# Finer transfers of w2, and the small loads cut so that the output's transfer takes the last of eight semaphores

## The chip, the cores and the metric

One core of one Trainium2 chip. The metric is device time of one execution in microseconds (us). The kernel before took 355.64 us (median of 3 executions, 355.63 to 355.8). Every execution also has a span (first to last instruction; 1.7 to 3.1 us shorter) and a mean granted TensorE clock. One execution of each kernel leaves a trace, and all trace times below are counted from the start of its span. PE is TensorE, DVE VectorE, ACT ScalarE and SP the sync engine. A transfer has landed when the last of the DMA engines that carry it has reported. The hidden vector is `relu(h @ w1)`, and the drain is the sync engine's first instruction after its final waits.

## The reference

One decode step of an adaptive-norm block: the modulation vectors come from `c`, attention reads a cache of 32768 keys and values for 8 groups of heads, and a small feed-forward layer follows.

```python
mod = (silu(c) @ w_mod).reshape(1, 6, 1, -1)        # sa, ca, ga, sb, cb, gb
h = layernorm(x) * (1 + ca) + sa
x = x + ga * attention(h, k_cache, v_cache, wq, wo)  # 8 groups, 32768 x 128 each, bf16
h = layernorm(x) * (1 + cb) + sb
x = x + gb * (relu(h @ w1) @ w2)                     # 512 -> 1792 -> 512
```

Nine tenths of the 149.42 MB that are read (134.2 MB) are the cache. The weights w1 and w2 (1.8 MB each) are read last.

## The kernel before

All loads go through one queue, issued by the sync engine (SP) in a fixed order: w_mod (`wm`), c, x, wq, then K and V, wo, w1, w2. Four large buffers in SBUF go round. The parts that the change and the argument touch:

```python
# w2 in six transfers: (first row pair, row pairs, which rows of the pair); FB = 2, FA = 7
W2P = [(0, 2, slice(0, FB)), (2, FA - 5, slice(0, FB)), (FA - 3, 1, slice(0, FB)), (FA - 2, 1, slice(0, FB)),
       (FA - 1, 1, slice(0, 1)), (FA - 1, 1, slice(1, FB))]
W1P = [(0, KT - 1), (KT - 1, KT)]
# ... cut ...
w2_v = B_w2.rearrange("(a p b) d -> p a b d", p=P, b=FB)   # pair a: 256 KB, 2 KB on each partition
# ... cut ...
wm_sb = need(("wm",))
cx_row = const.tile([16, D // 8], BF16)
stream_dma(cx_row[0:8], c[0].rearrange("(a n) -> a n", a=8))
stream_dma(cx_row[8:16], A_x[0, 0].rearrange("(a n) -> a n", a=8))
# ... cut: attention, projection, second norm, w1 ...
for part, (base, n, bs) in enumerate(W2P):
    w2_sb = need(("w2", part))          # each part's first matmul waits for that part's transfer
    for a in range(n):
        for b in range(bs.start, bs.stop):
            ft = (base + a) * FB + b
            for i in range(KT):         # 4 matmuls per row tile, 56 in all
                nc.tensor.matmul(ffn_ps, lhsT=hid_bd[:, ft, i, :], rhs=w2_sb[:, a, b - bs.start, i*P:(i+1)*P], ...)
# two vector operations, then
nc.sync.dma_start(out=out[0, 0].rearrange("(i n) -> i n", i=KT), in_=o_bf[:])
```

Two rules are not in the code but in the built program. Each transfer takes the next of eight semaphores in turn, and waits until the transfer eight before it has landed. And the program ends with six waits of the sync engine on all semaphores, in a fixed order: 2; 3 and 1; 4 and 0; 5; 6; 7.

## Time and profile before

| | before |
|---|---|
| time | 355.64 us |
| span of the profiled execution | 353.7 us |
| DMA queue, share of 16 engines | 98.4% |
| PE / DVE busy | 79% / 59% |
| last transfer of w2 landed | 350.20 |
| last matmul started | 350.49 |
| output landed, then drain of the sync engine | 352.531, 352.845 |

The kernel is bound by the bytes it reads. The prediction shows the lines for that.

### The profile page before, as it was taken

How to read it: one execution, taken by the hardware profiler on the slowest of the kernel's cores; microseconds unless marked ns; L12 is line 12 of the kernel's file. 1: busy time of each engine (PE TensorE's matmuls, PEld its weight loads, DVE VectorE, ACT ScalarE, POOL GpSimd, SP SyncE). 2: the span in 40 equal slices, each digit the busy share in tenths (PEclk: the TensorE clock that was granted, in tenths of full speed). 3: DMA queues.
4: the chain of work that ended last, by engine and by line, in shares of the span. 5: the costliest groups of instructions: out<-in, count | busy, mean ns of one | idle time of the engine just before them, and what ended most of it. 6: DMA issues, size and time to landing. Idle time of an engine off the chain costs nothing. (4 is left out here: it accounts for less than half of the span.)

```text
span 353.7 us, 4064 instructions
## 1 busy us (share of the span) xinstructions
PE 278.1 (79%) x1348; PEld 111.8 (32%) x1351; DVE 207.3 (59%) x269; ACT 28.2 (8%) x68; POOL 8.5 (2%) x14
## 2 busy tenths in 40 slices
PE   0352781999898979897969797979789787989995
PEld 0121230333343423332323233333333233334445
DVE  8555774882868268472949177553938095743050
ACT  1212004000110011001100101010100010020000
POOL 9000000000000000000000000000000000000000
PEclk9995997799899999999999998999999999999999
DMA  8999999999999999999999999999999999999994
GB/s 317 450 419 452 432 412 437 448 419 424 459 419 422 445 437 421 437 441 419 437 448 419 424 459 416 426 436 437 422 434 445 426 424 448 430 422 422 423 418 186
DMA packets 7076, 149.59 MB, mean 423 GB/s; under 512 B 792, under 2 KB 1048, under 8 KB 2200
## 3 DMA queue, kind: packets, MB, share of 16 engines
q1 hardware_dynamic: 7064, 149.43, 98.4%
q8 instruction: 8, 0.13, 0.1%
q14 instruction: 4, 0.03, 0.0%
HBM read 149.42 MB, written 0.00 MB: 422 GB/s over the span
## 5 line engine op out<-in xcount | busy, mean ns | idle before, releaser
L411 DVE STREAM_TRANSPOSE KTt<-Ksb 128x2048 f32<-128x2048 f32 x64 | 143.2, 2283 | 66.5 <-DMA Ksb<-in_A_k_cache_dram 58.8
L493 PE MATMUL o_ps<-Vsb,PT_g 128*16 (+1 forms) x512 | 128.0, 382 | 22.4 <-ACT qbd L395 9.5
L431 PE MATMUL S_ps<-KTt,qbd 128*128 128x512 bf16 x512 | 122.5, 391 | 22.2 <-DVE KTt L411 20.6
L431 PEld LDWEIGHTS <-qbd 128*128 128x128 bf16 x512 | 49.0, 98 | 87.0 <-issue 29.1
L493 PEld LDWEIGHTS o_ps<-Vsb,PT_g 128*16 x416 | 35.9, 86 | 90.7 <-issue 66.4
L437 DVE TENSOR_SCALAR_CACHE_REDUCE S_g<-S_ps 128x512 f32<-128x512 f32 x16 | 11.0, 690 | 27.7 <-PE S_ps L431 27.7
L395 ACT COPY qbd<-qrep_sb 32x128 bf16<-32x128 bf16 x32 | 9.4, 295 | 139.0 <-PE S_ps L431 137.9
L474 DVE STREAM_TRANSPOSE PT_g<-P_g 128x1024 bf16<-128x1024 bf16 x8 | 9.7, 1218 | 6.6 <-ACT P_g L468 6.6
L465 ACT ACTIVATE nbias<-Mb_ps 128x1 f32<-128x1 f32 x8 | 1.4, 171 | 131.1 <-PE Mb_ps L463 131.1
L493 PEld LDWEIGHTS <-PT_g 128*16 128x16 bf16 x96 | 8.2, 90 | 11.0
L233 PE MATMUL xc_ps<-cx_sel,cx_bd 16*128 16x2 bf16 x4 | 0.3, 172 | 12.8 <-DVE cx_bd L227 12.8
L468 ACT ACTIVATE P_g<-S_g,nbias 128x1024 bf16<-128x1024 f32 x8 | 9.2, 1148 | 0.2
L524 DVE SCALAR_TENSOR_TENSOR Y<-o_ps,smask,Y 16x128 f32<-16x128 f32 x24 | 8.1, 339 | 0.8
L179 DVE COPY sel<-ident_bf 128x128 bf16<-128x128 bf16 x4 | 7.6, 3730 | 0.0
L480 PE MATMUL L_ps<-Lexp,ones_f 128*128 128x4 f32 x16 | 3.0, 257 | 4.3 <-DVE Lexp L477 4.3
L606 PE MATMUL spare_ps<-qbd,ident_bf 128*128 128x512 bf16 x16 | 5.1, 380 | 0.2 <-issue 0.2
L449 PE MATMUL mT_ps<-ident_f,m_p 128*1 128x128 f32 x8 | 2.2, 270 | 3.9 <-DVE m_p L446 2.0
L452 DVE TENSOR_REDUCE Mrow<-mT_ps 1x4 f32<-1x128 f32 x8 | 2.1, 257 | 5.3 <-PE mT_ps L449 5.3
L480 PEld LDWEIGHTS L_ps<-Lexp,ones_f 128*128 128x128 f32 x16 | 3.1, 222 | 5.7 <-issue 5.1
L543 DVE TENSOR_TENSOR oT_sb<-acc_ps,Linv 128x4 bf16<-128x4 f32 x8 | 1.2, 151 | 5.7 <-PE acc_ps L530 5.7
L514 DVE MEMSET o_ps<- 16x512 f32 x8 | 3.9, 485 | 0.8
L561 DVE CAST o_sb<-o_ps 128x4 bf16<-128x4 f32 (+2 forms) x4 | 0.7, 166 | 6.1 <-PE o_ps L557 6.1
(112 smaller groups left out, 85.2 us busy)
## 6 DMA issues: line engine op xcount, KB each, us to landing
Ksb<-in_A_k_cache_dram SPq DMA_DIRECT2D x16, 4096.0 KB, 29.2
Vsb<-in_A_v_cache_dram SPq DMA_DIRECT2D x15, 4096.0 KB, 24.5
wq_sb<-in_A_wq_dram SPq DMA_DIRECT2D x1, 4096.0 KB, 18.8
Vsb<-in_A_v_cache_dram SPq DMA_DIRECT2D x2, 2048.0 KB, 23.4
wm_sb<-in_w_mod_dram SPq DMA_DIRECT2D x1, 3072.0 KB, 10.4
wo_sb<-in_A_wo_dram SPq DMA_DIRECT2D x1, 2048.0 KB, 25.1
w_sb<-in_B_w_dram SPq DMA_DIRECT2D x1, 1344.0 KB
wo_sb<-in_A_wo_dram SPq DMA_DIRECT2D x1, 1024.0 KB, 27.0
```

Source lines behind the costliest of these rows:

```text
L179: nc.vector.tensor_copy(out=sel[:, hp, :].rearrange("p (a c) -> p a c", a=4), in_=src)
L395: nc.scalar.copy(out=o, in_=i)
L411: t = nc.vector.transpose(out=KTt[:].bitcast(F32), in_=Ksb[:, 32 * half:32 * half + 32, :].rearrange("p j d -> p (j d)").bitcast(F32),)
L431: nc.tensor.matmul(S_ps_tiles[g], lhsT=qbd[g % 2][:, hp, s, :], rhs=KTv[:, 16 * sl:16 * sl + 16, h, :, par], start=(t4 == 0 and sl == 0 an ...
L437: nc.vector.tensor_scalar(out=S_tiles[g][:, G, :], in0=S_ps_tiles[g], scalar1=1.0, scalar2=None, op0=ALU.mult, op1=ALU.max, accum_out=m_ti ...
L468: nc.scalar.activation(out=P_g[:], in_=S_g[:].rearrange("p g f -> p (g f)"), func=ACT.Exp, bias=nbias[:], scale=scale, accum_out=l_g[:],)
L474: nc.vector.transpose(out=PT_g[:], in_=P_g[:])
L480: nc.tensor.matmul(L_ps[:], lhsT=ones_f[:], rhs=Lexp[:], start=True, stop=True)
L493: nc.tensor.matmul(o_tiles[g][:], lhsT=PT, rhs=Vx, start=False, stop=False, skip_group_check=True)
L514: nc.vector.memset(o_tiles[g][:], 0.0)
L524: nc.vector.scalar_tensor_tensor(out=Y[:], in0=o[:, s], scalar=smask[:, s:s + 1], in1=Y[:], op0=ALU.mult, op1=ALU.add,)
L606: nc.tensor.matmul(spare[0], lhsT=ident_bf[:], rhs=qbd[0][:, 0, 0:4, :], start=True, stop=True)
```

## The change

The intent: matmuls of w2 can begin on each row pair as it lands, and the output's transfer is the 56th, so that its semaphore is the last one that the final waits ask for.

```diff
-    W2P = [(0, 2, slice(0, FB)), (2, FA - 5, slice(0, FB)), (FA - 3, 1, slice(0, FB)), (FA - 2, 1, slice(0, FB)),
-           (FA - 1, 1, slice(0, 1)), (FA - 1, 1, slice(1, FB))]
+    W2P = [(a, 1, slice(0, FB)) for a in range(FA - 1)]
+    W2P += [(FA - 1, 1, slice(b, b + 1)) for b in range(FB)]
...
-    stream_dma(cx_row[0:8], c[0].rearrange("(a n) -> a n", a=8))
-    stream_dma(cx_row[8:16], A_x[0, 0].rearrange("(a n) -> a n", a=8))
+
+    for at, row in ((0, c[0]), (8, A_x[0, 0])):
+        rows = row.rearrange("(a n) -> a n", a=8)
+        for a0, a1 in ((0, 3), (3, 6), (6, 8)):
+            stream_dma(cx_row[at + a0:at + a1], rows[a0:a1])
```

## The prediction

> **What bounds the kernel now.** I read the page from its second part down. The DMA row of the forty slices says which resource is full, and it is full nearly everywhere:
>
> ```profile
> DMA  8999999999999999999999999999999999999994
> ...
> q1 hardware_dynamic: 7064, 149.43, 98.4%
> ```
>
> The reader is to see that the sixteen DMA engines are nine tenths busy or more in 38 of 40 slices, and that the one queue through which all loads go fills 98.4% of them. The table of stretches (columns: bounds and length of the stretch, busy time of PE, PEld, DVE, ACT, POOL with instruction counts, granted clock, DMA share, GB/s) gives the rate between start-up and tail:
>
> ```profile
> 20.00:340.00 320.00, 262.54 (x1146) 102.00 (x1145) 190.30 (x219) 23.99 (x61) 0.00 (x0) 0.96 1.00 431
> ```
>
> DMA share 1.00 at 431 GB/s, while PE works 262.54 of 320 us. So nothing that only starts a load earlier helps in the middle: the bytes (149.42 MB) set the time. What the change can touch is the first 20 us and the last few. The chain that ended last shows those:
>
> ```profile
> 305.94 25.65 DMA Vsb<-in_A_v_cache_dram
> 331.59 0.02 issue
> 331.61 16.67 DMA w_sb<-in_B_w_dram
> 348.28 0.04 issue
> 348.32 2.41 PE ffn_ps L742 x40
> 350.73 0.02 issue
> 350.75 0.29 DVE o_rows L747
> ```
>
> Loads until 348.28, then 40 matmuls without a stop, two vector operations, the output. The timeline of the tail says the same of PE:
>
> ```profile
> 347.11 1.05 PE L742 MATMUL ffn_ps<-w_sb,hid_bd 128*4 128x128 bf16 x16 [0.47 <-ACT hid_bd L728]
> 348.32 2.39 PE L742 MATMUL ffn_ps<-w_sb,hid_bd 128*4 128x128 bf16 x40 [0.15 <-DMA w_sb<-in_B_w_dram]
> ...
> 351.37 0.29 SPq L750 DMA_DIRECT2D out_dram<-o_bf  x1
> ```
>
> The first 16 matmuls (the first w2 transfer, two row pairs) wait for the hidden vector; the other 40 start when the second transfer, again two row pairs, has landed. 2.39 us for 40, the last lasting 0.219 us, is a pitch of (2.39-0.219)/39 = 0.0557 us.
>
> Last come the waits of the sync engine after the output is issued (instruction, count, duration in ns as minimum/median/maximum, start of first and last). The first answer is for 351.6 to 353 us, the second for 352.58 to 352.83:
>
> ```profile
> L776 SPq EVENT_SEMAPHORE  x6: 17/28/783, 351.7 to 352.8; - x6
> ```
>
> ```profile
> L776 SPq EVENT_SEMAPHORE  x4: 28/28/28, 352.6 to 352.8; - x4
> ```
>
> Six waits; the 783 ns one holds the output's landing (351.77 to 352.55), and four more follow it although their transfers landed long before.
>
> **What the Trainium skill says.** "DMA: Bandwidth & Descriptors", section "Bandwidth", under where its 436 GB/s comes from, puts the ceiling of the sixteen ports at 435.2 GB/s. The trace agrees: 431 over the middle 320 us, and a 4096 KB load lands every 9.68 us, or 433 GB/s. The same page, "Rules for kernel authors", asks for 1 MiB or more per transfer and calls anything under 64 KB mostly overhead. The pieces here are 256 KB. The landing records (16 per transfer, the last one counts) show that this costs little when transfers queue behind each other: the two 256 KB pieces of w2 landed 0.64 and 0.60 us after their predecessors, and 256 KB at 433 GB/s would be 0.605. The page's "Why a DMA increments its semaphore by 16 and not by 1" says that the number of engines a transfer uses must divide its outer dimension: 8 partitions ran on 8 engines (the trace has 8 landings for c, agreeing); 3 would run on 3. "Perfetto Trace Analysis", "Sequencer-only Instruction", says that the recorded window of such an instruction leaves its semaphore wait out. Here the trace differs: the wait on two semaphores has the 783 ns in its record.
>
> **The change part by part.** Transfers take eight semaphores in turn. Before, there are 50 (wm, c, x, wq, 33 of K and V, 4 of wo, 2 of w1, 6 of w2, output), and the output, number 49 from zero, has semaphore 49 mod 8 = 1. After, there are 56, and the output has 55 mod 8 = 7. The compiled programs end in the same list of waits: semaphore 2, then 3 with 1, 4 with 0, 5, 6, 7. So the output's wait moves from second to last.
>
> 1. *Final waits.* Before, the wait for the output ends at 352.553 and the drain behind it starts at 352.845; four waits lie between, at a pitch of 0.06 us. After, the drain follows at once, 0.04 us later as it does before after its last wait. Saved: 0.292 - 0.04 = 0.25 us. No other engine is awaited there (PE's drain starts at 350.25, DVE's at 351.08), so it counts in full.
>
> 2. *PE in the tail.* w2 lands (last engine) at 346.98, 348.28, 348.92, 349.52, 349.85, 350.20. PE leaves the last byte 0.29 us late: its final matmul starts at 350.494, although four matmuls after 350.20 plus the usual 0.04 us would put it at 350.24 + 3 x 0.0557 = 350.41. It is late because it idled from 348.00 to 348.32 waiting for two row pairs at once. With single pairs the third lands near 347.63, before PE is free, and PE runs on; it then waits for the sixth (349.56), has done it at 350.01, the next half at 350.23, and starts the last at 350.24. Saved: 0.09 us.
>
> 3. *The w2 stream.* The two 512 KB transfers took 1.32 and 1.30 us, the singles 1.24 per 512 KB. If all go at the singles' pace, 2.62 - 2 x 1.24 = 0.14 us; two more completions may take some of it back. I choose half: 0.07 us.
>
> 4. *Head.* Four more issues at about 0.37 us put wq's issue at about 3.4 us instead of 1.93; the engines are busy with wm until 10 to 11.1. The semaphores' turn makes the first K load wait for wm (landed 11.14) where it was issued at 2.33, but wq fills the queue until 20.77. The third K load still waits for PE (issued 18.68), with work queued to 40.97. The vector engine waits for six transfers with two more wait instructions of about 0.05 us, and the last x piece may land near 11.5 instead of 10.87; at most some 0.2 us on a chain with twenty to spare. Cost: 0. Do the small pieces cost the engines they run on (0 and 1 get six, before two)? The mean landing from wm to wq is 9.68 us apart with c and x between, and 9.68 from wq to the first K load without, so I count none.
>
> Sum: 0.25 + 0.09 + 0.07 = 0.41 off 355.64, or 355.23.
>
> **The rivals.** *A new wait starves the queue at the end.* Transfers 53 and 54, w2's last halves, wait for the semaphores of numbers 45 and 46, which are now w1 (landed 344.60 and 345.66), where before they waited for wo (340.11, 341.41). The issue moves about 4.3 us later. Against: at 345.7 w2's whole pairs are still queued until about 349.5, and even the output, on an idle queue, landed 1.16 us after its issue. If it starved, 1 to 2 us more: about 357. Unlikely.
>
> *Each transfer costs its engines something.* If two more in the tail and four small ones in front on the slowest engines cost 0.05 to 0.1 us each, part 3 vanishes and 0.2 to 0.4 comes on top: 355.4 to 355.7. The landing pitches speak against it, but halves of 128 KB took 0.33 and 0.35 where 0.30 would do.
>
> *The tail is the DMA's alone.* Parts 2 and 3 give nothing and the waits only: 355.39.
>
> *The engines' skew moves.* The first and last engine finish 1.96 us apart, built up in steps of 0.5 us on single engines; if a step falls elsewhere, the end moves by some tenths either way.
>
> **Range and chances.** I put the estimate at 355.25, a shade above the sum because the second rival takes rather than gives. The runs of before lie within 0.17 us. The range is 354.95 (parts 2 and 3 in full, a step lost) to 355.6 (waits gained, most of it spent on transfers). Two per cent is 7.1 us, far outside: within 2% 0.99, faster 0.003, slower 0.007.
>
> **What would show it.** After the output's landing no wait of the sync engine is left, and the drain starts within 0.05 us. The 40 matmuls split into runs that begin without a gap after the first 16, then halt briefly for the last three transfers; PE ends within 0.45 us of the last landing. Issues of w2's last two halves come near 344.6 and 345.7. Wrong would be: last landing later than about 350.3, or DMA below nine tenths in the slices of the first 40 us.

## More of the kernel before

`keep_clock(n)` issues n dummy matmuls in the tail, there to keep TensorE's clock up.

```profile
PEclk9995997799899999999999998999999999999999
```

A slice is 8.8 us. There are dips in the first eleven slices and a small one (8) in the 25th; from the 26th on, the last 133 us, every slice is 9, which is full.

## The result, and the profile after

The changed kernel took 355.37 us (median of 6, 355.2 to 356.22); the kernel before took 355.77 us in the same rounds (median of 6, 355.63 to 357.04). The ratio is 0.9988, with a 95% interval of 0.997 to 1.0005: the same within 2%. A ratio here is the mean time of one kernel's executions over that of the other's of the same rounds, so it is not quite the ratio of the medians quoted. All executions on one core counted, but for one that the last job shows.

The profiled execution is not a typical one: it took 355.93 us, while four of the other five took 355.2 to 355.42. This has to be kept in mind in what follows. The middle is unchanged. From the page's third part and from the table of stretches, kernel after:

```profile
q1 hardware_dynamic: 7096, 149.43, 98.3%
```

```profile
20.00:340.00 320.00, 262.87 (x1136) 102.68 (x1135) 190.02 (x216) 24.03 (x61) 0.00 (x0) 0.95 1.00 432
```

The same bytes at 432 GB/s (431 before), DMA share 1.00. The head is as predicted. The sync engine's issues, kernel after (start, length from first to last issue of the group, transfer, count):

```profile
3.11 0.36 SPq L139 DMA_DIRECT2D wq_sb<-in_A_wq_dram  x1
11.40 7.81 SPq L139 DMA_DIRECT2D Ksb<-in_A_k_cache_dram  x3
```

wq goes out at 3.11 instead of 1.93, and the first K load at 11.40 instead of 2.33, when wm has landed; wq landed at 21.03 (20.77 before), the first K load at 30.72 (30.45): nothing ran dry.

The final waits are as intended. The sync engine's waits from 352.45 to 353.37 us, kernel after:

```profile
L779 SPq EVENT_SEMAPHORE  x6: 17/28/28, 352.5 to 353.3; - x6
```

Five are over before the output lands at 353.31; the sixth is the output's own and none is left behind it. The drain starts at 353.39, 0.08 us after the landing, where the kernel before needed 0.31.

The tail itself is another matter. The chain of waits, kernel after:

```profile
307.44 7.16 PE S_ps L434 x32
...
347.85 0.30 ACT hid_bd L731
348.15 0.04 issue
348.20 3.30 PE ffn_ps L745 x56
351.52 0.29 DVE o_rows L750
```

and its timeline:

```profile
348.20 3.29 PE L745 MATMUL ffn_ps<-w_sb,hid_bd 128*4 128x128 bf16 x56 [0.21 <-ACT hid_bd L731]
...
352.14 0.29 SPq L753 DMA_DIRECT2D out_dram<-o_bf  x1
```

Before, the chain ran over the transfers; here it starts at 307.40 us and has no transfer in it, only PE and short steps of other engines between. The last w2 transfer had landed at 350.27, as before, but the hidden vector came at 347.85 instead of 346.73, and 56 matmuls in one go then took until 351.49. By then it made no difference in how many pieces w2 had come. The clock row of this page shows something that the row of before does not have:

```profile
PEclk9996997799899999999999998999999996999999
```

A 6 in the 34th slice. The trace's clock records have half clock from 295.7 to 302.5 us. The table of stretches for just that time, first the kernel before, then the kernel after (third column: PE busy and, in brackets, matmuls; behind POOL: clock, DMA share, GB/s):

```profile
295.70:302.50 6.80, 6.03 (x27) 2.29 (x26) 1.07 (x5) 0.00 (x0) 0.00 (x0) 1.00 0.98 424
```

```profile
295.70:302.50 6.80, 6.14 (x17) 2.38 (x16) 1.09 (x5) 0.00 (x0) 0.00 (x0) 0.50 0.96 414
```

PE is as busy in both, but does 17 matmuls instead of 27. It catches up in part; 1.1 us is left at the tail.

### The profile page after: what moved, and what is told of

Same layout as the page of the kernel before. It is cut to its first block, busy times and chain, and to the rows that moved or that the text cites. A ratio compares the mean times of both kernels' runs of the same rounds, so it can differ in the third digit from the quotient of the medians. Undisturbed runs are those within 1.5% of the kernel's fastest.

```text
span 354.2 us, 4075 instructions
## 1 busy us (share of the span) xinstructions
PE 279.4 (79%) x1351; PEld 112.6 (32%) x1351; DVE 207.6 (59%) x269; ACT 28.3 (8%) x68; POOL 8.5 (2%) x14
## 5 line engine op out<-in xcount | busy, mean ns | idle before, releaser
L609 PE MATMUL spare_ps<-qbd,ident_bf 128*128 128x512 bf16 x19 | 5.9, 380 | 0.0
L304 PE MATMUL mod_ps<-wm_sb,siluT 128*1 128x512 bf16 x24 | 3.6, 624 | 1.0 <-DVE siluT L298 1.0
```

The lines of the kernel that those rows point to most:

```text
L304: nc.tensor.matmul(dst[j // 4][32 * (j % 4):32 * (j % 4) + 1, :], lhsT=src_T[:, kt:kt + 1], rhs=w[:, kt, j * 512:(j + 1) * 512], start=(kt ...
L609: nc.tensor.matmul(spare[0], lhsT=ident_bf[:], rhs=qbd[0][:, 0, 0:4, :], start=True, stop=True)
```

## The experiments

Twelve runs were made, in four jobs, each job on another chip. Every job timed the kernel before again, as the last column of the table shows (the jobs' own kernel before). The second column has the number of transfers of w2, the number of c and x together, and the waits that come after the output's own. All times in us; "hidden" is the start of the operation that writes the hidden vector.

| run | w2 / c and x / waits after | hidden | last w2 landed | last matmul starts | landing to drain | median (range) | before, same job |
|---|---|---|---|---|---|---|---|
| before | 6 / 2 / 4 | 346.73 | 350.20 | 350.49 | 0.31 | 355.64 (355.63-355.8) | |
| after | 8 / 6 / 0 | 347.85 | 350.27 | 351.27 | 0.08 | 355.37 (355.2-356.22) | 355.77 |
| r_after | 8 / 6 / 0 | 347.88 | 350.27 | 351.30 | 0.08 | 355.79 (355.42-356.05) | 356.38 |
| e_waits | 6 / 8 / 0 | 349.79 | 353.28 | 353.55 | 0.08 | 358.9 (358.13-359.67) | 356.38 |
| e_w2 | 8 / 2 / 4 | 348.10 | 350.52 | 351.52 | 0.34 | 355.94 (355.63-356.43) | 356.38 |
| e_cx3 | 6 / 6 / 2 | 347.95 | 350.36 | 351.37 | 0.21 | 355.91 (355.34-356.26) | 356.38 |
| r_before | 6 / 2 / 4 | 346.81 | 350.28 | 350.58 | 0.31 | 355.52 (355.28-356.3) | 356.13 |
| e_waits2 | 6 / 6, and 2 unused / 0 | 347.07 | 350.54 | 350.84 | 0.08 | 356.04 (355.44-356.63) | 356.13 |
| e_w14 | 14 / 2 / 4 | 348.31 | 351.75 | 351.96 | 0.31 | 356.75 (356.2-357.6) | 356.13 |
| e_nospare | 8 / 6 / 0 | 346.71 | 350.51 | 351.38 | 0.08 | 356.21 (356.04-357.69) | 356.13 |
| r_after2 | 8 / 6 / 0 | 348.21 | 350.62 | 351.63 | 0.08 | 355.86 (355.25-356.3) | 356.14 |
| e_early | 8 / 6 / 0 | 348.86 | 350.62 | 354.79 | 0.08 | 358.13 (355.56-359.47) | 356.14 |
| e_thin | 8 / 6 / 0 | 347.25 | 350.43 | 351.55 | 0.08 | 356.62 (356.21-357.38) | 356.14 |
| e_lean | 8 / 6 / 0 | 347.14 | 350.64 | 350.87 | 0.08 | 355.2 (355.13-355.54) | 355.97 |

**r_after**: the changed kernel unedited.

> The changed kernel again, unedited. Its first profiled execution took 355.93 us although most of its other executions took 355.2 to 355.42; in it the hidden vector came 1.1 us later than before (348.15 against 347.03) while the last w2 transfer landed at 350.27. Theory A (that profile caught a stretch in which PE ran slower, and the change has nothing to do with it): most executions here within 355.15 to 355.45, and a profile of one of those has the hidden vector near 347.1, the last matmul start within 0.3 us of the last landing, and a drain within 0.1 us of the output's landing. Rival B (the change itself delays PE, for instance because PE meets more waits): the hidden vector is again near 348 in most profiles and the fastest executions are no faster than 355.6.

Ratio 0.9985 (0.9968 to 1.0002). The profile has half clock again, from 295.3 to 302.1, and PE late again. The executions run from 355.42 to 356.05, so neither expectation is met cleanly: the fastest is below rival B's 355.6, but three of six lie near 356. The question of what the half clock has to do with the change stayed open for r_before.

**e_waits**: the final waits alone, with a mistake in it.

```diff
-        for a0, a1 in ((0, 3), (3, 6), (6, 8)):
+        for a0, a1 in ((0, 2), (2, 4), (4, 6), (6, 8)):
# w2 as before
```

> w2 as before, in six transfers; c and x in four transfers each, so that there are 56 transfers and the output again has the last semaphore. Only the order of the final waits changes. Theory A (parts of the prediction add up: waits 0.25, PE in the tail 0.09): 0.25 us faster than before, about 355.4; landing to drain 0.08 us instead of 0.31; 40 matmuls without a stop from 348.3 as before. Rival (the gain is in the w2 pieces): no more than 0.1 us faster than before.

It was slower by 2.5 us (ratio 1.0076), which neither theory had. The sync engine's issues, kernel e_waits:

```profile
2.47 8.53 SPq L139 DMA_DIRECT2D cx_row<-in_A_x_dram  x4
11.04 0.36 SPq L139 DMA_DIRECT2D wq_sb<-in_A_wq_dram  x1
11.44 7.76 SPq L139 DMA_DIRECT2D Ksb<-in_A_k_cache_dram  x3
```

With wm and eight small pieces, the last piece of x is the ninth transfer. It takes wm's semaphore and so waits for wm, and wq stands behind it: 11.04 instead of 3.11. The wq load then landed at 23.20 instead of 21.03, the last w2 transfer at 353.28, and PE kept the pattern of before (40 matmuls in one go, the last starting 0.27 after the landing). The change just avoids this: wm, its six pieces and wq are exactly eight transfers. The drain came 0.08 us after the landing, as for the changed kernel.

**e_w2**: the w2 part alone.

```diff
+    W2P = [(a, 1, slice(0, FB)) for a in range(FA - 1)]
+    W2P += [(FA - 1, 1, slice(b, b + 1)) for b in range(FB)]
# c and x as before
```

> w2 in eight transfers, c and x as before: 52 transfers, the output has semaphore 3, whose wait is the second of six as before. Theory A: the final waits cost what they did (landing to drain 0.31 us), PE no longer idles before the third row pair, and the kernel is 0.05 to 0.15 us faster than before, about 355.55. Rival (starting transfers later, after w1 has landed, costs at the end): last landing 0.1 us or more later than 350.2 to 350.3 and the kernel no faster or slower than before.

Ratio 0.999 (0.9973 to 1.0007). Landing to drain is 0.34, near the 0.31 expected. The rest cannot be judged: this execution had the half clock too (295.7 to 302.5), and PE came late. The transfers can be judged, for they do not wait for PE here: from the second part of w1 to the last of w2 they took 345.96 to 350.52, or 4.56 us; the kernel before took 345.66 to 350.20, or 4.54.

**e_cx3**: c and x alone.

```diff
+        for a0, a1 in ((0, 3), (3, 6), (6, 8)):
# w2 as before
```

> c and x in three transfers each, w2 as before: 54 transfers, the output has semaphore 5, whose wait is the fourth of six, so two waits follow it instead of four. Theory A (each wait that follows costs 0.06 us): 0.12 us faster than before, half of what e_waits gains, about 355.5; landing to drain 0.2 us. Rival (the pieces of c and x in front cost time on two engines): not faster, or slower by 0.1 us or more, with the last landing later.

Ratio 0.9987 (0.997 to 1.0005), half clock at 295.7. The sync engine's waits behind the output's, kernel e_cx3, 353.46 to 353.59 us:

```profile
L779 SPq EVENT_SEMAPHORE  x2: 28/28/28, 353.5 to 353.5; - x2
```

Two waits are left, and landing to drain is 0.21 us. With 0.31 for four and 0.08 for none, each wait is worth 0.06 us.

**r_before**: the kernel before unedited, as a control.

> The kernel before, unedited, as a control. Four profiles of the kernels with more transfers showed a stretch of half clock from 295.7 to 302.5 us, after which the hidden vector came at 347.9 to 348.1 instead of 346.7; the only profile of the kernel before showed none. Theory A (the stretch falls into some executions of every kernel): the times spread as widely as those of the others, about 355.5 to 357.3; ratio 1.000 within its interval; if the profiled execution has the stretch, the hidden vector is late by about 1.1 us here too, the span is near 354.5, and the 40 matmuls follow the 16 without a gap. Rival B (more transfers bring the stretch about): no such stretch in the profile and nearly all executions at 355.5 to 355.8.

The profile had no half clock after 221 us, and everything in its tail repeats the first profile within 0.1 us. The times fit theory A: 355.28 to 356.3 here and 355.35 to 357.25 for the same kernel's other eleven executions of this job. What matters more: its ratio to itself is 0.9985 (0.9967 to 1.0003). That is as far from 1 as the changed kernel's 0.9988, 0.9985 and 0.9987. So the ratios alone do not show that the change is faster, and the argument has to rest on records inside the traces.

**e_waits2**: e_waits without its mistake.

```diff
# on e_cx3, in load():
+        if key == ("k", 4, (0, 1)):
+            for i in range(2):
+                unused = const.tile([8, D // 8], BF16, name=f"unused{i}")
+                stream_dma(unused[:], c[0].rearrange("(a n) -> a n", a=8))
```

> e_waits again without its mistake. There, with wm and eight pieces of c and x, the last piece was the ninth transfer and waited for wm (issued at 10.77), wq behind it was issued at 11.04 instead of 3.1, and the engines ran dry for some 3 us. Here c and x go in three transfers each and two unused loads of 1 KB follow in the middle of the stream, so that there are again 56 transfers and the output has the last semaphore, with w2 as before. Theory A (final waits alone): 0.2 to 0.25 us faster than before; landing to drain 0.08 us; last landing 350.2 to 350.4. Rival (the waits' gain is lost to the small transfers): not faster than before by more than 0.05 us.

Landing to drain 0.08 us, as expected. The time does not show it: ratio 0.9995 (0.9977 to 1.0014), and the last landing in the profile was 350.54, later than expected. Over the traces the last landing of kernels without a stall varies from 350.20 to 350.64, more than the 0.2 to 0.25 us looked for, so the total time is no measure of the waits; the record of the wait is. What follows that landing can be compared: from it to the drain, 2.43 us here and 2.40 in e_waits, against 2.64 and 2.66 in the two traces of the kernel before, with PE in time in all four.

**e_w14**: w2 in fourteen transfers.

```diff
+    W2P = [(a, 1, slice(b, b + 1)) for a in range(FA) for b in range(FB)]
# c and x as before
```

> w2 in fourteen transfers of 128 KB, c and x as before: 58 transfers, the output has semaphore 1 again, so the final waits are those of before. It prices transfers in the tail. Theory A (a transfer more costs its engines 0 to 0.04 us as long as others queue behind it): last landing at most 0.3 us after that of before (350.2 to 350.5), time within 0.2 us of before. Rival (later issue starves the queue: the last seven pieces are each issued when the piece eight before has landed on the slowest engine, with 2.3 us of data behind it): gaps of more than 0.4 us between the last landings, last landing 1 us or more later, 356.5 or more.

Last landing 351.75, and 5.58 us from the second part of w1 to it (346.17 to 351.75) instead of 4.54: the rival holds. The landing records split the sum. The first eight pieces, 1 MB, took 2.75 us; before, the first two transfers, also 1 MB, took 2.62. That is 0.13 us for six more transfers, or 0.02 each. The other 0.75 MB took 2.83 us instead of 1.92, and there the sixteen engines' landings of one piece, 2.3 us apart up to the sixth, draw together to 0.6 to 0.9. The first landing of each piece had come 0.33 to 0.37 us after that of the piece before; for the seventh and eighth it came 0.98 and 1.05 us after: the engines that run ahead had run out of work. The end of the chain, kernel e_w14, says the same:

```profile
348.97 2.78 DMA w_sb<-in_B_w_dram
351.75 0.04 issue
351.79 0.40 PE ffn_ps L741 x4
```

The last piece was issued at 348.97 and landed 2.78 us later; in the changed kernel, 345.73 and 350.27, 4.5 us.

**e_nospare**: the changed kernel without dummy matmuls.

```diff
-        keep_clock(...)          # all ten places of the tail, 19 matmuls
```

> The changed kernel without the 19 dummy matmuls of its tail, which take 0.22 to 0.38 us each on PE. In executions with the late stretch of half clock PE, not the transfers, sets the end, and some of the dummy matmuls are in its chain (3.9 us of it by the profile). Theory A (PE-bound when the stretch comes late): the slow executions become faster, the median falls by 0.3 to 0.8 us and the hidden vector comes at most as late as 347.4, unless the clock falls in the tail without them. Rival (the clock falls without them, or the chain waits elsewhere): median unchanged or up to 2 us slower, with a granted clock of 0.5 in the last 15 us.

The hidden vector came at 346.71, 3.81 us ahead of the last landing and so earlier than in any trace with dummies (3.49 at most): they do lie in PE's path. How much of the 1.1 us against the changed kernel is theirs is not shown, for this execution had only 3.4 us of half clock at 295 us, not 6.8; the expectation of e_early overlooks that. And the clock fell in the tail. Stretches of kernel e_nospare:

```profile
342.00:347.00 5.00, 3.17 (x74) 2.53 (x71) 1.87 (x13) 0.59 (x2) 0.00 (x0) 0.59 1.01 400
347.00:352.00 5.00, 4.54 (x56) 4.35 (x56) 0.33 (x2) 0.00 (x1) 0.00 (x0) 0.73 0.45 167
```

0.59 and 0.73 instead of 1.00; the last 56 matmuls, 3.29 us in the changed kernel, took 4.54. Median 356.21: no gain.

**r_after2**: the changed kernel a third time.

> The changed kernel once more, for a profile without the stretch of half clock near 295 us, which is still missing. Theory A (by the prediction's steps, when the stretch is absent): PE idles between the first 16 and the other matmuls for none of the time or only at the last three transfers, the last matmul starts 0.21 us after the last landing instead of 0.30, the drain starts 0.08 us after the output's landing, span 353.3 to 353.5. Theory B (more transfers bring the stretch about): the stretch is there again, for the fifth time in five profiles of kernels with w2 in eight transfers or c and x in six next to it, and most spans lie near 354.2.

Half clock at 295.8 once more, PE late once more, but three of six spans at 353.3, 353.5 and 353.8. The lowest span of the kernel before is 353.5.

**e_early** and **e_thin**: fewer dummies.

```diff
# e_early: the nine dummies ahead of project(3) removed, the ten behind it kept
# e_thin:  every keep_clock(2) and keep_clock(3) of the tail becomes keep_clock(1): 11 of 19 left
```

> The changed kernel without the nine dummy matmuls ahead of the last projection; the ten behind it stay. In e_nospare the hidden vector came 1.1 us earlier than in the changed kernel although the stretch was there, but the clock then fell to 0.59 from 342.9 us on. Theory A (the nine lie in PE's chain when the stretch comes late, and do nothing for the clock behind them): where the stretch is there, the hidden vector comes at 347.2 or before and the clock stays at 1.00 in the tail; median 0.2 to 0.5 us below the changed kernel of the same job, and no execution over 355.6. Rival (the clock looks back over them): half clock again from about 343 us, and a median above the changed kernel's.

> The changed kernel with each group of two or three dummy matmuls in the tail cut to one: 11 instead of 19 remain, spread as before. Theory A (some dummies at every place keep the clock): as e_early, the median 0.1 to 0.4 us below the changed kernel of the same job, clock 1.00 in the tail. Rival (the clock needs PE nearly full): half clock from about 343 us, median 0.3 us or more above it.

Both rivals hold. Stretch of kernel e_early:

```profile
342.00:347.00 5.00, 4.76 (x41) 2.30 (x42) 1.96 (x13) 0.29 (x1) 0.00 (x0) 0.50 1.00 396
```

Half clock from 340.9 to 354.5, median 358.13. e_thin had half clock from 346.1 to 349.5, median 356.62. In the eleven traces with all dummies no half clock falls between 303 and 353 us. The dummies earn their place; no better version came from here.

**e_lean**: the changed kernel with five matmuls of PE's work left out (its result is off; it is an experiment, not a version to use).

```diff
-        pv(LAST, (3,))
+        pv(LAST, (3,), range(11))
```

> The changed kernel with five of the 32 matmuls of the last group's last values left out (a slightly wrong result, on purpose), so that PE reaches the tail 1.1 us (5 x 0.22) earlier even in an execution with the stretch of half clock near 295 us; all transfers stay as they are. It tests the prediction's part 2, which no profile has shown yet, because PE was late in each profile of the changed kernel. Theory A (part 2 as predicted once PE is in time): hidden vector 3.2 us or more ahead of the last landing, the last matmul starts 0.21 us after the last landing (four matmuls behind it) where the kernel before has 0.29 and 0.30; drain 0.08 us after the output's landing; spans 353.3 to 353.6 in most executions, with few above 354. Rival 1 (the pieces give nothing: PE ends 0.3 us after the last landing also here). Rival 2 (the clock falls for want of work on PE, as in e_early and e_thin: half clock from about 341 to 346 us and spans over 355).

This execution had no half clock after 226 us, so PE was in time anyway. It is the one trace with w2 in eight transfers, the final waits of the change, and PE in time. Timeline, then chain, of kernel e_lean:

```profile
347.49 3.60 PE L745 MATMUL ffn_ps<-w_sb,hid_bd 128*4 128x128 bf16 x56 [0.21 <-ACT hid_bd L731]
```

```profile
350.00 0.04 issue
350.04 1.07 PE ffn_ps L745 x16
```

All 56 matmuls run as one group with 0.3 us of halts in it, without the gap of before behind the first 16. The chain goes over the sixth pair's landing (350.00) and the 16 matmuls behind it; the last starts at 350.87, 0.24 us after the last landing. Before and r_before had 0.29 and 0.30. The five executions lie within 355.13 to 355.54, spans 353.2 to 353.8, and none is late. Ratio 0.9976 (0.9962 to 0.999). One of the kernel before's executions in this job took 1520.76 us; it is left out.

## Why the prediction was right

The measured 355.37 lies in the range, near the 355.25 predicted, and within 2% was right. The hit on the number is in part luck. The range (354.95 to 355.6) was drawn from three executions of the kernel before that lay within 0.17 us; over all jobs its executions took 355.28 to 357.31 (one of 1520.76 apart). The changed kernel's other two medians, 355.79 and 355.86, lie outside the range, and the unchanged kernel's control median, 355.52, inside it. So the steps have to be judged, not the number.

*Final waits (predicted 0.25).* Right: landing to drain fell from 0.31 in both traces of the kernel before to 0.08 in all nine traces with no wait after the output's, so 0.23 us; two waits left gave 0.21. Nothing but the order of six instructions changed there. The missing 0.02 is the output's own wait: it ends 0.02 us after the landing before and 0.04 after it in the changed kernel.

*PE in the tail (predicted 0.09).* The mechanism was right, the size too large: 0.24 us from last landing to last matmul instead of 0.29 to 0.30, so 0.06. In e_lean the two halves landed within 0.64 us of the sixth pair, less than PE needs for its 12 matmuls (0.67), so PE still had work in hand at the last landing. This part is shown by e_lean alone, and only where PE is in time. In the three traces of the changed kernel PE was not: it ended 1.2 us after the last landing, where the prediction's sign was 0.45, and the 56 matmuls did not split.

*The w2 stream (predicted 0.07).* This term was mis-sized. The step took the difference between pairs (1.31 us per 512 KB) and singles (1.24) for a gain of single pairs. Once all went singly, the stretch from w1 to the end took 4.55 to 4.57 us in all eight traces, against 4.51 to 4.55 in the five with six transfers: the pairs were not slow because they were pairs. Measured: 0.02 lost, not 0.07 saved.

*Head (predicted 0).* Right as far as the traces tell: wq landed at 20.81 to 21.12 in the three traces of the changed kernel, at 20.77 and 20.91 in the two of the kernel before. The second rival's price is 0.02 us per transfer in e_w14. But there is no margin: wm, six pieces and wq are eight transfers, and in e_waits two pieces more cost 2.5 us.

The sum of what was measured is 0.23 + 0.06 - 0.02, about 0.27 us in an execution with PE in time and 0.23 in one with PE late; predicted were 0.41. From the last landing of w2 to the drain e_lean took 2.36 us, the kernel before 2.64 and 2.66. Over all executions of unedited kernels the medians are 355.97 (53 of before, without the one of 1520.76) and 355.75 (18 of after), 0.22 apart; the means are 0.39 apart. As the control's ratio shows, the times alone could not have told either from nothing.

*What the prediction did not see* is the stretch of half clock. It took PE's arrival for a constant. In the five profiles of three kernels with 6.8 us of half clock at 295 us and w2 or c and x as in the change (after, r_after, r_after2, e_w2, e_cx3), the hidden vector came 2.39 to 2.42 us ahead of the last w2 landing; in the five without (before, r_before, e_waits, e_waits2, e_lean) 3.47 to 3.49. Then PE sets the end, about 0.7 us later, and part 2 is worth nothing. e_waits2 had half clock from 257 to 264 without harm: its hidden vector came 3.47 ahead. So part of the spread between executions comes from such a stretch: the five had spans of 354.2 to 354.7, and four of the others 353.7 to 353.8 (e_waits apart). Another part lies outside the span: the changed kernel's slowest execution of the first job, 356.22 us, had a span of 353.4.

Does the change bring the stretch about? All six profiles of kernels with w2 in eight or fourteen pieces, or c and x in six without unused loads, that kept their dummies and all of PE's work, had it; the two of the kernel before had not. But that grouping leaves out e_early and e_lean, which have the whole change, differ only after 302 us, and had no half clock there. The clock records allow a closer look. All clock changes of a trace lie on a grid of 3.413 us, whose place differs from execution to execution. And PE has the same halt in both kernels just before, kernel r_before, then kernel after:

```profile
294.48 1.90 PE L431 MATMUL S_ps<-KTt,qbd 128*128 128x512 bf16 x8 [1.74 <-DVE KTt L411]
```

```profile
294.44 2.42 PE L434 MATMUL S_ps<-KTt,qbd 128*128 128x512 bf16 x8 [1.74 <-DVE KTt L414]
```

Twelve traces have this halt of 1.74 us (e_waits and e_waits2 halted 1.35 and 1.41 and had no half clock there). In the eight in which the next edge of the grid fell 0.27 to 1.24 us after PE started again, half clock began at that edge; in the four in which it fell 1.37 to 2.25 us after (before, r_before, e_early, e_lean), there was none. So what divides the profiles is where the grid fell, and the changed kernel's own three differ in that (0.82, 1.03, 1.24). This is read from the records and was not tested by a run; that the change moves the grid is not excluded, but nothing shows it. The kernel before has executions with spans of 354.2 or more in every later job, the length of a late PE, but no trace of such a one was caught.

*The rival of the starved queue* did not happen in the change (the last two pieces were issued at 344.67 and 345.73, as predicted, and landed 0.34 and 0.30 us after their predecessors), but e_w14 shows that it was no idle worry: with fourteen pieces the last 0.75 MB took 0.9 us longer.

## What to carry to other kernels

When semaphores are taken in turn, the number of transfers decides two things that no line of the program names: who waits for whom eight transfers later, and how many waits stand behind the last landing; count them in the built program, and count before adding even one small transfer. A gain of a quarter of a microsecond is to be read from the record that holds it, with the unchanged kernel run as a control of the times. And where two limits lie within a microsecond of each other, look at the clock row before taking the arrival of the second as given.

## What the Trainium skill lacked or had wrong

- "Perfetto Trace Analysis", "Sequencer-only Instruction": it says that the recorded window leaves the semaphore wait out. One wait of the kernel before, on two semaphores with the output's named second, has 783 ns in its record. Where the output's is named first (the changed kernel), the record has 28 ns, as the page says. So the wait for the second of two semaphores appears to be inside the record.
- "DMA: Bandwidth & Descriptors": no price of one more transfer in a full queue. Here it was 0.02 us for 128 KB pieces on all partitions (2.75 against 2.62 us for 1 MB with six transfers more), as long as the queue stayed full; its rule of 1 MiB or more per transfer asks for more than was needed in that case, where 128 KB pieces were 5% slower than 512 KB ones.
- The same page gives no size for how far the sixteen engines run apart in a long stream: here one transfer's landings spread over 2 us at the end (348.24 to 350.20), and the last one counts. In e_w14 a short queue starved the leading engines first.
- "TensorE: Matmul & The Clock Gate", Part 1, has the half clock in windows of about 3.4 us that run free of the kernel's start. The traces agree (stretches of 3.41, 6.83, 10.24 and 13.65 us; matmuls 0.0557 and 0.107 us apart). It has no figure for a halt shorter than a window: here, after one of 1.74 us, half clock followed or not by where the window's edge fell (up to 1.24 us after PE's restart, or from 1.37 us on).
- No page gives the cost of an instruction that waits for what is already met: 0.06 us each on the sync engine.
